# Last rows of wo on half of the partitions, results in two transfers, semaphores cleared, last K in halves

## The chip, the cores and the metric

The kernel runs on one core of a Trainium2 chip. The metric is the device time of one execution, in microseconds (us), lower is better. Before the change three runs took 1300.05, 1300.1 and 1302.17 us; the median is 1300.1 us.

## The reference

One decode step for two tokens (B = 2) of width 512: attention over a cache of 8192 keys in 32 heads of 128, times a gate that comes from a small MLP, plus the input.

```python
def _A_ref(x, k_cache, v_cache, wq, wo):          # x [2,1,512], caches [2,32,8192,128] float32
    q = (x @ wq).reshape(B, Sq, H, Dh).transpose(0, 2, 1, 3)
    scores = jnp.einsum("bhqd,bhkd->bhqk", q, k_cache) * (Dh ** -0.5)
    p = _softmax(scores, axis=-1)
    o = jnp.einsum("bhqk,bhkd->bhqd", p, v_cache)
    return o.transpose(0, 2, 1, 3).reshape(B, Sq, H * Dh) @ wo      # wo [4096, 512]

def _B_ref(x, w1, b1, w2, b2):
    y = _layernorm(x)
    h = _gelu(jnp.einsum("bsd,df->bsf", y, w1) + b1)
    return jnp.einsum("bsf,fd->bsd", h, w2) + b2

xn = _layernorm(x)
return x + _A_ref(xn, k, v, wq, wo) * _silu(_B_ref(xn, w1, b1, w2, b2))
```

All of it is float32. The two caches are 512 MiB together, and each of their values is used once.

## The kernel before

**Blocks.** The 64 pairs of token and head are worked on two at a time: 32 blocks (`N`, index n), each with one K tile and one V tile of 128 partitions x 16384 floats, which is 8 MiB. Half of the partitions belongs to each head of the pair. K tiles alternate between two buffers (`kb[0]`, `kb[1]`); V tiles go to one buffer (`vb`). In the last block V goes to `kb[1]` instead, in two halves (lines 606 to 608), because the wo matrix then needs `vb`.

**One block.** VectorE (DVE) multiplies the K tile with the query, in place and in two halves of 64 keys for each partition (`scores_mul`, L524), and sums each half over the head's 128 values (`scores_sum`, L531). The largest score of each head is found by DVE (L535), turned by TensorE (PE, L538) and reduced again (L541). ScalarE (ACT) takes the exponentials (L552). PE multiplies them with the V tile (`weighted`, L569: 32 matmuls of 512 columns, each of which is two passes in the trace), ACT copies the sums out of PSUM (L574), PE folds them (L576), and DVE spreads them into a matrix `Z` (L582). Blocks are staggered: the V product of block n-1 runs while DVE works on the scores of block n. Blocks 1 to 30 are a hardware loop; the first and the last are written out.

**Transfers.** All large loads are issued by SyncE (SP), in one queue and in the order of the program (`load`, L314). Each waits until its buffer is free: a K load for the scores of the tile before it, a V load for the matmuls of the block before. `load_k` (line 316) takes K tile 0 in two halves, each with a semaphore of its own, so that DVE can start on the first half; all the other K tiles are one transfer. An edit to `load_k` also changes the semaphores' names.

**Order of the work.** `Plan` records every operation with what it reads and writes. It adds the waits that follow from that and writes out each engine's instructions in program order. [...]

**The end (lines 611 to 660).** Once the last V product of `vb` is done, wo is loaded into `vb`: partition p holds rows 32p to 32p+31, 2 KB each. "Column c" below is row 32p+c of every partition, 128 rows and 256 KB in all. The 32 columns come in five transfers, `wo0` to `wo4`, with columns 0-15, 16-25, 26-29, 30 and 31. After the last block, PE and DVE make the normalised attention output `on` (L624 to L629), 128 partitions x 32 columns for each token. The product with wo then has three parts:

- columns 0 to 25 by one matmul of 512 output columns each, summed in four PSUM strips (`wide`, L639), which ACT copies out (L642);
- columns 26 to 29 by four matmuls of 128 output columns each, straight into the final layout (`acc`, L648);
- four matmuls that fold `wide` into `acc` (L653), then columns 30 and 31 as the four before (L648).

DVE multiplies with the gate (L657) and adds x (L658), and SP writes the result with one transfer (L659, 4 x 2 x 128 floats). `emit` ends SP's instructions with a wait for that transfer (L125). Nothing clears the kernel's semaphores.

Of the kernel before, what the change touches and what calls it, by code (L numbers as in the profile page):

```python
# [21 lines left out]
class Plan:  # L22
# [63 lines left out]
    def emit(self, heads):  # L86

        nc = self.nc
# [28 lines left out]
        for e in self.eng:  # L117
            ops = [o for o in self.ops if o.eng == e]
            inside = [j for j, o in enumerate(ops) if o.loop]
            if not inside:  # L120
                for o in ops:
                    put(o, order(o.waits))
                if e == "sp":

                    nc.sync.wait_ge(sems[("dma", "out")], told[("dma", "out")])  # L125
                continue
            for o in ops[:inside[0]]:
                put(o, order(o.waits))
# [32 lines left out]
            for o in ops[inside[-1] + 1:]:  # L161
                put(o, order(o.waits))


def decode_kernel(nc, x, kc, vc, wq, wo, w1, b1, w2, b2, out):
    P = 128
# [17 lines left out]
    RM = RB * (B - 1) + 1  # L184
    PH = P // H
    OC = DH // PH
    UP = U * PH


# [9 lines left out]
    def pe(fn, r=(), w=(), it=None, loop=False):  # L199
        op("pe", fn, r, w, it=it, loop=loop)  # L200

    def dve(fn, r=(), w=(), it=None, loop=False):
        op("dve", fn, r, w, it=it, loop=loop)

    def act(fn, r=(), w=(), it=None, loop=False):
        op("act", fn, r, w, it=it, loop=loop)
# [4 lines left out]
    def sbuf(name, shape):  # L211
        return nc.alloc_sbuf_tensor(name, shape, F32).ap()
# [39 lines left out]
    RS = sbuf("rs", [P, 1])  # L252
    O4 = sbuf("o4", [P, JW * DH])
    q_nat = O4
    rl = sbuf("rl", [P, B])
    on = sbuf("on", [P, RM, OC])

# [45 lines left out]
    def bank():  # L303
        i = turn[0] % 4
        turn[0] += 1
        return scratch[i], f"s{i}"
# [6 lines left out]
    def load(dst, src, sem, w, over=()):  # L313
        op("sp", lambda: nc.sync.dma_start(dst, src), (), w, over=over, dma=sem)  # L314

    def load_k(n):
        i = (n + 1) % 2
        if n == 0:
            for s in range(2):
                load(kbuf[i][:, s * M:(s + 1) * M], kf[n][:, s * M:(s + 1) * M], f"k{s}", [("kb", i, s)])  # L320
            return
        load(kbuf[i], kf[n], f"kb{i}", [("kb", i, s) for s in range(2)])


    WO_PIECES = (0, 16, 26, 30, 31, 32)
    WIDE = WO_PIECES[2]


    load(w1_sb, w1.rearrange("(p c) f -> p c f", p=P), "w1", ["w1"])
# [51 lines left out]
    for j in range(QT):  # L381
# [6 lines left out]
                                        axis=AX.X, op=ALU.add), ["ident"], ["mod"])  # L388
    dve(lambda: nc.vector.tensor_reduce(out=blk, in_=ident.rearrange("p (j r) -> p j r", r=R),
                                        axis=AX.X, op=ALU.add), ["ident"], ["blk"])  # L390
    layernorm(y, xn, "y", "xn", 1)
    transposed(xnT[:, :, (NQ - 1) * B:NQ * B], xn, "xnT", "xn")
    transposed(yT, y, "yT", "y")
# [214 lines left out]
                load(kbuf[1][:, s * M:(s + 1) * M], vf[N - 1][:, s * M:(s + 1) * M], f"v1{s}", [("kb", 1, s)])  # L608


    wo_r = wo.rearrange("(p c) n -> p c n", p=P)
    for i, (a, e) in enumerate(zip(WO_PIECES, WO_PIECES[1:])):
        load(wo_sb[:, a:e], wo_r[:, a:e], f"wo{i}", [("wo", i)], over=["vb"])
# [19 lines left out]
    def piece(c):  # L633
        return ("wo", max(i for i, a in enumerate(WO_PIECES[:-1]) if a <= c))


    for c in range(WIDE):
        j = c % QT
        pe(lambda c=c, j=j: matmul(wide[R * j:R * j + RM, :], on[:, :, c], wo_sb[:, c, :],  # L639
                                   start=(c < QT), stop=(c + QT >= WIDE)), ["on", piece(c)], ["wide"])  # L640
    w4 = O4
    act(lambda: nc.scalar.copy(w4, wide), ["wide"], ["o4"])  # L642

# [1 line left out]
    def rows(lo, hi):  # L645
        for c in range(lo, hi):
            for j in range(QT):
                pe(lambda c=c, j=j: matmul(acc[R * j:R * j + RM, :], on[:, :, c], wo_sb[:, c, j * P:(j + 1) * P],  # L648
                                           start=(c == WIDE), stop=(c == OC - 1)), ["on", piece(c)], ["acc"])

    rows(WIDE, WO_PIECES[3])
    for j in range(QT):
        pe(lambda j=j: matmul(acc[R * j:R * j + RM, :], mod[:, :RM], w4[:, j * P:(j + 1) * P], start=False, stop=False),  # L653
           ["mod", "o4"], ["acc"])
    rows(WO_PIECES[3], OC)

    dve(lambda: nc.vector.tensor_mul(gate, acc, gate), ["acc", "gate"], ["gate"])  # L657
    dve(lambda: nc.vector.tensor_add(gate, gate, x4), ["gate", "x4"], ["gate"])  # L658
    op("sp", lambda: nc.sync.dma_start(out.rearrange("b o (j n) -> j (b o) n", n=P), gate[::RB, :]),  # L659
       ["gate"], dma="out")  # L660

    plan.emit(HEADS)

# [24 lines left out]
```

## Time and profile before

| What | Value |
|---|---|
| Median of three runs | 1300.1 us |
| The profiled execution | 1300.12 us |
| Its span, first to last instruction | 1298.4 us |
| DVE busy | 1134.7 us (87%) |
| PE busy (matmul) | 406.5 us (31%) |
| ACT busy | 77.6 us (6%) |
| Read from HBM | 559.30 MB, 431 GB/s over the span |
| Last instruction of `acc` ends | 1295.92 us |
| SP issues the result | 1296.63 us, takes 0.70 us |
| SP sees it landed | 1298.41 us |

Times in traces count from the first instruction of the profiled execution. The 1.7 us between its span and its time lie ahead of the first and behind the last instruction. PE's matmuls are pipelined: the start of a pass and the distance to the next one say how fast PE goes, while a pass of 512 columns shows 0.59 us of its own. "PEclk" is the share of the full TensorE clock that the chip granted.

The load of a transfer is shared by up to 16 DMA engines. Each reports the end of its share, so the trace has as many completion marks for a transfer as engines took part (one more when fewer than 16 do), and the transfer has landed at the last of them.

| Transfer | Issued at | First mark | Last mark (landed) |
|---|---|---|---|
| K of block 31 | 1194.42 | 1235.03 | 1236.95 |
| V of block 30 | 1227.53 | 1254.38 | 1256.32 |
| V of block 31, first half | 1227.90 | 1264.09 | 1266.02 |
| V of block 31, second half | 1233.10 | 1273.81 | 1275.73 |
| wo0, 16 columns | 1265.66 | 1283.52 | 1285.46 |
| wo1, 10 columns | 1266.03 | 1289.62 | 1291.56 |
| wo2, 4 columns | 1266.50 | 1292.10 | 1294.06 |
| wo3, 1 column | 1266.99 | 1292.79 | 1294.67 |
| wo4, 1 column | 1267.45 | 1293.45 | 1295.30 |

### The profile page before, as it was taken

To read this page: it belongs to the slowest core of one execution; us is meant where nothing else is said; L and a number is where in the kernel's file an instruction comes from. 1 tells how busy PE (TensorE), PEld (TensorE's weight loads), DVE (VectorE), ACT (ScalarE), POOL (GpSimd) and SP (SyncE) were. 2 spreads that over 40 slices of the span, in tenths; PEclk is the share of its full clock that TensorE was granted. 3 is DMA by queue.
4 is the path that set the end of the run, shared out by engine and by line. 5 is a ranking of instruction groups with operands and counts; after the bars stand their busy time and mean duration, and the time that the engine had idled before them with its cause. 6 is when DMAs were issued, how large, how long until landed. Compare 5 with 4: busy or idle time off the path is not lost.

```text
span 1298.4 us, 6747 instructions
## 1 busy us (share of the span) xinstructions
PE 406.5 (31%) x2708; PEld 122.9 (9%) x2708; DVE 1134.7 (87%) x276; ACT 77.6 (6%) x250; POOL 1.4 (0%) x8
## 2 busy tenths in 40 slices
PE   5502333312333311333321333321333321233336
PEld 1100011000101000101100101000101100001102
DVE  3599999888889988889988888988888988888982
ACT  1100000000000000000000000000000000000000
POOL 0000000000000000000000000000000000000000
PEclk9856666556666556666555666655666655666658
DMA  9999999999999999999999999999999999999998
GB/s 404 447 423 444 426 438 432 424 444 428 440 428 432 440 424 444 426 440 430 426 442 428 442 428 434 436 424 444 426 442 428 428 444 424 442 428 436 434 422 358
DMA packets 10682, 559.39 MB, mean 431 GB/s; under 512 B 1192, under 2 KB 1200, under 8 KB 1460
## 3 DMA queue, kind: packets, MB, share of 16 engines
q1 hardware_dynamic: 10668, 559.29, 99.6%
q8 instruction: 4, 0.07, 0.0%
q14 instruction: 2, 0.02, 0.0%
q10 hardware_dynamic: 8, 0.01, 0.0%
HBM read 559.30 MB, written 0.00 MB: 431 GB/s over the span
## 4 chain that ended last, share of the span: by engine, by line
DMA 73%; PE 25%; DVE 1%; issue 0%; ACT 0%; SPq 0%; DVEq 0%
DMA vb<-in_A_v_cache_dram 71%; PE po L569 22%; DMA vb<-in_A_wo_dram 2%; PE s L410 1%; PE po L482 1%; PE s L452 0%; PE wide L639 0%; PE s L412 0%; DVE vb L418 0%; PE acc L648 0%; ACT L431 0%; DVE vb L356 0%; PE s L459 0%; DVE vb L367 0%; DVE vb L444 0%
## 5 line engine op out<-in xcount | busy, mean ns | idle before, releaser
L524 DVE TENSOR_TENSOR kb<-kb,Q 128x8192 f32<-128x8192 f32 x64 | 555.6, 8681 | 109.8 <-DMA kb<-in_A_k_cache_dram 100.5
L531 DVE TENSOR_REDUCE sc<-kb 128x64 f32<-128x8192 f32 x64 | 552.3, 8666 | 0.0
L569 PE MATMUL po<-vb,PZ 128*8 128x512 f32 x1984 | 287.6, 745 | 292.5 <-DMA vb<-in_A_v_cache_dram 292.5
L547 PE MATMUL s<-nm,srow 1*128 1x2 f32 x64 | 18.6, 358 | 368.5 <-DVE nm L541 368.5
L569 PEld LDWEIGHTS po<-vb,PZ 128*8 128x8 f32 x1984 | 57.0, 104 | 497.0 <-issue 494.4
L538 PE MATMUL s<-ident,mx 128*1 128x128 f32 x32 | 11.9, 373 | 186.3 <-DVE mx L535 186.3
L547 PEld LDWEIGHTS s<-nm,srow 1*128 1x128 f32 x64 | 15.9, 307 | 378.0 <-DVE nm L541 378.0
L574 ACT COPY o<-po 128x512 f32<-128x512 f32 x32 | 18.7, 585 | 539.1 <-PE po L569 539.1
L548 ACT COPY bias<-s 128x2 f32<-128x2 f32 x32 | 5.1, 160 | 620.3 <-PE s L547 620.3
L576 PE MATMUL s<-mod,o 128*128 128x2 f32 x256 | 33.7, 254 | 22.8 <-ACT o L574 22.8
L576 PEld LDWEIGHTS s<-mod,o 128*128 128x128 f32 x256 | 31.0, 191 | 52.5 <-ACT o L574 52.5
L552 ACT ACTIVATE PZ<-sc,bias 64x128 f32<-64x128 f32 x64 | 25.5, 399 | 1.8
L538 PEld LDWEIGHTS s<-ident,mx 128*1 128x1 f32 x32 | 2.5, 79 | 189.8 <-DVE mx L535 159.1
L582 DVE TENSOR_TENSOR Z<-blk,s 128x8 f32 (+1 forms) x32 | 5.2, 163 | 12.4 <-PE s L576 12.4
L418 DVE COPY vb<-vb 2x384 f32<-2x384 f32 x4 | 1.8, 502 | 15.1 <-ACT vb L414 15.1
L410 PE MATMUL s<-vb 128*2 128x512 f32 (+1 forms) x24 | 11.7, 638 | 0.3 <-ACT vb L375 0.3
L552 ACT ACTIVATION_READ_ACCUMULATOR PZ<-sc,bias 64x1 f32 x64 | 11.8, 185 | 0.0
L535 DVE TENSOR_REDUCE mx<-sc 128x1 f32<-128x128 f32 x32 | 9.2, 286 | 1.1
L556 ACT ACTIVATE ZR<-half,rs 128x8 f32 (+1 forms) x32 | 9.7, 302 | 4.1
L541 DVE TENSOR_REDUCE nm<-s 1x2 f32<-1x128 f32 x32 | 8.7, 272 | 0.4 <-PE s L538 0.4
L569 PE MATMUL po<-kb,PZ 128*8 128x512 f32 x64 | 8.5, 694 | 1.4 <-ACT PZ L552 1.4
L657 DVE TENSOR_TENSOR gate<-acc,gate 128x128 f32<-128x128 f32 x1 | 0.3, 291 | 9.6 <-PE acc L648 9.6
(86 smaller groups left out, 78.8 us busy)
## 6 DMA issues: line engine op xcount, KB each, us to landing
kb<-in_A_k_cache_dram SPq DMA_DIRECT2D x2, 4096.0 KB, 49.2
kb<-in_A_v_cache_dram SPq DMA_DIRECT2D x2, 4096.0 KB, 40.4
vb<-in_B_w_dram SPq DMA_DIRECT2D x2, 2752.0 KB, 12.7
vb<-in_A_wo_dram SPq DMA_DIRECT2D x1, 4096.0 KB, 19.8
vb<-in_A_wo_dram SPq DMA_DIRECT2D x1, 2560.0 KB, 25.5
vb<-in_A_wo_dram SPq DMA_DIRECT2D x1, 1024.0 KB, 27.6
vb<-in_A_wo_dram SPq DMA_DIRECT2D x2, 256.0 KB, 27.8
kb<-in_A_k_cache_dram SPq DMA_DIRECT2D x31, 42.6
```

The costliest lines, as they stand in the source:

```text
L410: pe(lambda f=f, w=w, ph=ph, c=c: matmul(ph[:B, :w], yT[:, c, :], w1_sb[:, c, f:f + w], start=(c == 0), stop=False), ["yT", "w1"], [k])
L482: pe(lambda i=i, c=c, wv=wv, a=a, j=j, hd=hd: matmul(PO[R * j:R * j + NQ * B, :].rearrange("m (h d) -> m h d", d=DH), xnT[:, c, a:a + NQ * ...
L524: vector(n, n, lambda n: nc.vector.tensor_tensor(out=k, in0=k, in1=cols(Q, n * DH, DH).unsqueeze(1).to_broadcast([P, M, DH]), op=ALU.mult) ...
L531: vector(n, n, lambda n: nc.vector.tensor_reduce(out=SC[:, s * M:(s + 1) * M], in_=k, axis=AX.X, op=ALU.add), [("kb", i, s)], [("sc", s)])
L535: vector(n, n, lambda n: nc.vector.tensor_reduce(out=MX, in_=SC, axis=AX.X, op=ALU.max), [("sc", 0), ("sc", 1)], ["mx"])
L538: pe(lambda i: transpose(PM[:1, :P], MX, ident), ["mx", "ident"], ["s1"], it=n, loop=n > 0)
L547: pe(lambda i: matmul(PN[:, :U], srow, NM, start=True, stop=True), ["srow", "nm"], ["s2"], **one)
L552: act(lambda i, r=r, s=s: nc.scalar.activation(PZ[r, :, s, :], sc[r], AF.Exp, bias=BIAS[r, s:s + 1], scale=SCALE, accum_out=RS[r]), ["bias ...
L556: act(lambda i: nc.scalar.activation(cols(ZR, i * UP - UP, UP), half, AF.Copy, scale=RS), ["half"] + [("rs", s) for s in range(U)], [("ZR" ...
L569: pe(lambda i, t=t, j=j, v=v: matmul(PO[R * j:R * j + U * JW, :], PZ[:, t].rearrange("p s j -> p (s j)"), v[:, t * JW:(t + 1) * JW, :].rea ...
L574: act(lambda i: nc.scalar.copy(O4, PO), ["po"], ["o4"], **one)
L576: pe(lambda i, k=k: matmul(PT[:, :U], O4[:, k * DH:(k + 1) * DH], mod[:, k:U * JW:JW], start=(k == 0), stop=(k == JW - 1)), ["o4", "mod"], ...
```

## The change

- **wo.** Column 31 is no longer the last transfer. It is loaded ahead of the others by two transfers `wx0` and `wx1` (128 KB each) into 64 partitions of the query buffer `Q`, which is free once DVE has multiplied the last K tile. The source is written with a leading dimension of 8. `wo0` to `wo4` now hold columns 0-15, 16-24, 25-28, 29 and 30. As the 64 partitions hold other rows than `on` does, two small matmuls with a selection matrix `pick2` (made once at the start by a DVE copy) bring the matching values into 64 partitions, ACT copies them to `on2`, and two matmuls of 512 columns join the `wide` sum behind columns 0 to 15.
- **Results.** One transfer for each token, one issued by SP and one by ACT, 4 x 128 floats each.
- **Semaphores.** SP waits for both and then clears the kernel's semaphores.
- **Last K.** K tile 31 is loaded in two halves, as K tile 0 is.

```diff
-                if e == "sp":
-                    nc.sync.wait_ge(sems[("dma", "out")], told[("dma", "out")])
...
+        ids = sorted(s.num for s in sems.values())
+        for k in sorted(k for k in sems if k[0] == "dma" and k[1].startswith("out")):
+            nc.sync.wait_ge(sems[k], told[k])
+        nc.sync.sem_clear(range(ids[0], ids[-1] + 1))
...
+    HALF = P // 2
+    EG = 8
...
+    wx = Q[:HALF, :2 * D].rearrange("p (t n) -> p t n", t=2)
+    on2 = sbuf("on2", [HALF, 2, RM])
+    pick2 = sbuf("pick2", [P, 2, HALF])
...
-        if n == 0:
+        if n in (0, N - 1):
             for s in range(2):
-                load(kbuf[i][:, s * M:(s + 1) * M], kf[n][:, s * M:(s + 1) * M], f"k{s}", [("kb", i, s)])
+                load(kbuf[i][:, s * M:(s + 1) * M], kf[n][:, s * M:(s + 1) * M], f"k{i}{s}", [("kb", i, s)])
...
-    WO_PIECES = (0, 16, 26, 30, 31, 32)
+    WO_PIECES = (0, 16, 25, 29, 30, 31)
     WIDE = WO_PIECES[2]
+    LAST = OC - 1
...
+    dve(lambda: nc.vector.tensor_copy(pick2.rearrange("p t (k r) -> p t k r", r=EG),
+                                      ident.rearrange("p (k t r) -> p t k r", t=2, r=EG)), ["ident"], ["pick2"])
...
+    wl = wo.rearrange("(k t r c) n -> t k r c n", t=2, r=EG, c=OC)
+    for t in range(2):
+        load(wx[:, t, :], wl[t, :, :, LAST, :], f"wx{t}", [("wx", t)],
+             over=[("Q", k) for k in range(2 * D // (NB * DH))])
...
-    for c in range(WIDE):
-        j = c % QT
-        pe(lambda c=c, j=j: matmul(wide[R * j:R * j + RM, :], on[:, :, c], wo_sb[:, c, :],
-                                   start=(c < QT), stop=(c + QT >= WIDE)), ["on", piece(c)], ["wide"])
+    p2, k2 = bank()
+    for t in range(2):
+        pe(lambda t=t: matmul(p2[:HALF, t * RM:(t + 1) * RM], pick2[:, t], on[:, :, LAST], start=True, stop=True),
+           ["pick2", "on"], [k2])
+    act(lambda: nc.scalar.copy(on2, p2[:HALF, :2 * RM].rearrange("p (t m) -> p t m", t=2)), [k2], ["on2"])
+    first = [(on[:, :, c], wo_sb[:, c, :], ["on", piece(c)]) for c in range(WIDE)]
+    first[WO_PIECES[1]:WO_PIECES[1]] = [(on2[:, t, :], wx[:, t, :], ["on2", ("wx", t)]) for t in range(2)]
+    for i, (a, b, keys) in enumerate(first):
+        j = i % QT
+        pe(lambda i=i, a=a, b=b, j=j: matmul(wide[R * j:R * j + RM, :], a, b, start=(i < QT),
+                                             stop=(i + QT >= len(first))), keys, ["wide"])
...
-    rows(WO_PIECES[3], OC)
+    rows(WO_PIECES[3], LAST)
...
-    op("sp", lambda: nc.sync.dma_start(out.rearrange("b o (j n) -> j (b o) n", n=P), gate[::RB, :]),
-       ["gate"], dma="out")
+    for b in range(B):
+        eng = "sp" if b % 2 == 0 else "act"
+        op(eng, lambda b=b, eng=eng: plan.eng[eng].dma_start(
+            out[b, 0].rearrange("(j n) -> j n", n=P), gate[RB * b::R, :]), ["gate"], dma=f"out{b}")
```

## The prediction

> **What bounds the kernel now.** I read the page first, for what is busy all the time.
>
> ```profile
> span 1298.4 us, 6747 instructions
> ...
> DMA  9999999999999999999999999999999999999998
> ...
> q1 hardware_dynamic: 10668, 559.29, 99.6%
> ...
> DMA 73%; PE 25%; DVE 1%; issue 0%; ACT 0%; SPq 0%; DVEq 0%
> ```
>
> SP's queue keeps the 16 DMA engines moving for 99.6% of the span. DVE is the busiest compute engine (87%), but it waits 3.5 us for each K tile. The change leaves the bytes as they are, so it can only act on what comes before the first and after the last byte. The end is therefore read next, in the chain of waits from 1227 us on:
>
> ```profile
> 1266.03 25.53 DMA vb<-in_A_wo_dram
> 1291.56 0.04 issue
> 1291.60 2.79 PE wide L639 x19
> 1294.39 0.88 PE acc L648 x32
> 1295.26 0.22 PE acc L653 x7
> 1295.48 0.48 PE acc L648 x16
> ```
>
> From the landing of wo1 at 1291.56 PE goes on until 1295.92. The trace's completion marks show a second chain beside it, hardly shorter: wo4 lands at 1295.30 and PE loads the first weights of column 31 at 1295.41, so the last landing has 0.11 us to spare. The end is set by both.
>
> How unevenly the DMA engines finish is in the windows of the last microseconds (columns: stretch, its length, busy us of PE, PEld, DVE, ACT, POOL, granted clock, DMA share, GB/s):
>
> ```profile
> 1292.00:1293.00 1.00, 1.00 (x16) 0.36 (x10) 0.00 (x0) 0.00 (x0) 0.00 (x0) 1.00 1.05 410
> 1293.00:1294.00 1.00, 1.00 (x12) 0.18 (x4) 0.00 (x0) 0.00 (x0) 0.00 (x0) 1.00 0.48 178
> 1294.00:1295.00 1.00, 1.00 (x34) 0.89 (x32) 0.00 (x0) 0.57 (x1) 0.00 (x0) 1.00 0.13 49
> ```
>
> The share falls from all engines to two. The sixteen marks of wo4 lag behind its first (1293.45) by 0, 0.11, 0.16, 0.26, 0.28, 0.30, 0.38, 0.40, 0.51, 0.60, 0.75, 1.00, 1.03, 1.53, 1.58 and 1.85 us. Five engines are late by 1 us or more. The same lags stand in every V transfer for hundreds of microseconds, so an engine that fell behind stays behind.
>
> **wo over eight engines.** In this trace the number of engines is that of a transfer's leading rows: the result (4 rows) has four completions, x (2 rows) two. So wx, with a leading 8, goes over eight. One column (256 KB) over sixteen engines costs each 0.63 us (wo3 to wo4 lands 0.63 apart); the same bytes over eight cost each of these 1.26. In front of the last landing the eight loaded engines then have 1.26 - 0.63 = 0.63 us more work than before, the other eight 0.63 less. What that gives depends on who is late:
> - latest (1.85) loaded: last landing +0.63;
> - latest not loaded, but 1.53 or 1.58 is: 1293.45 + 1.58 + 0.63 = 1295.66, +0.36;
> - none of these three loaded: 0.63 less for the latest is 1294.67, but a loaded engine with lag 0.75 now ends at 1294.83, -0.47.
>
> The trace names no engine. The packets of x, b1 and b2, on one and two engines, can be followed to the engines with lags 0.60 and 0.75; if the small counts always take the same first engines, these two are loaded. Six more of fourteen are, and were the lags strewn by chance, the three cases had 0.43, 0.42 and 0.15. I take +0.36, from -0.47 to +0.63. If eight engines don't reach their full rate, wx costs up to twice as much (the bound is mine: half rate), +1.26 more.
>
> [...]
>
> **PE behind wo1.** `wide` has one column less to do after wo1: two passes of 0.107 us (at full clock the timeline has four weight loads of L639 every 0.43 us): -0.21 on the first chain. The two wx columns are added ahead of wo1, +0.43, and the selection (4 short passes of 0.03 as in L648, an ACT copy of 0.16 to 0.27 as L548 and L384) ahead of `wide`. PE has idled there for 1.38 us (1290.22 to 1291.56), which covers 0.43; without that cover it would cost in full. The selection is done while PE waits for wo0.
>
> **Last K in halves.** V of block 31 in halves takes 9.70 + 9.71 us between landings, whole tiles 19.35: +0.06 for all engines, on the path. For DVE it takes a wait away:
>
> ```profile
> 1233.10 0.29 DVE L535 TENSOR_REDUCE mx<-sc 128x1 f32<-128x128 f32 x1
> 1233.32 0.16 DVE L582 TENSOR_TENSOR Z<-blk,s 128x8 f32 x1
> 1236.98 8.69 DVE L524 TENSOR_TENSOR kb<-kb,Q 128x8192 f32<-128x8192 f32 x1 [3.50 <-DMA kb<-in_A_k_cache_dram]
> ...
> 1271.68 0.29 DVE L535 TENSOR_REDUCE mx<-sc 128x1 f32<-128x128 f32 x1
> ```
>
> The first half lands near 1227.3, so L524 starts at 1233.5, 3.45 us earlier; the second half is there at 1237, before DVE needs it at 1242.2. Everything to `on` follows: 1271.68 becomes 1268.2, L569 starts at 1271.3, its second half needs V landed at 1275.8 and PE is there at 1276.3, `on` is ready at 1283.0 instead of 1286.42. There the gain stops: wo0 lands at 1285.5 or later. It isn't on the path (0), and it has an effect of its own: PE stands still from 1282.5 until wo0.
>
> **PE's clock.** What such a rest does is in the windows of the clock's own 3.41 us steps:
>
> ```profile
> 1226.58:1229.99 3.41, 1.93 (x20) 0.97 (x8) 3.41 (x1) 0.58 (x1) 0.00 (x0) 1.00 1.02 442
> 1229.99:1233.41 3.42, 0.00 (x0) 0.00 (x0) 3.39 (x3) 0.00 (x0) 0.00 (x0) 0.50 1.06 460
> ...
> 1274.37:1277.78 3.41, 3.05 (x16) 0.64 (x20) 0.00 (x0) 0.52 (x3) 0.00 (x0) 0.50 1.05 452
> 1277.78:1281.19 3.41, 3.41 (x36) 0.83 (x32) 0.00 (x0) 0.00 (x0) 0.00 (x0) 1.00 1.02 437
> ...
> 1288.02:1291.43 3.41, 2.20 (x23) 0.54 (x14) 0.00 (x0) 0.00 (x0) 0.00 (x0) 1.00 0.92 388
> ```
>
> A step with PE busy for 1.93 us is followed by half clock, one with 2.20 is not; a step of 3.05 us at half clock brings full clock back. PE's rest of 3 to 4 us always leaves one step under 1.9. So `wide` starts at half clock, 0.213 us a pass (four of L569 every 0.85 us), and gets it back after 3.4 us (6 chances in 10 by where the steps lie) or 5.2 to 6.5: 1.7 us lost, or 2.6 to 3.2. With a late engine loaded (lag 1.66 at wo0), wo0 lands at 1283.52 + 1.66 + 1.26 + 0.06 = 1286.50. Then 36 passes are through at 1286.57 + 3.85 + 1.7 = 1292.1, wo1 is there (1291.95), 18 passes more take 1.93: the last starts at 1294.1 instead of 1293.80. First chain: +0.3, or up to +1.5 with the longer half clock. The last landing gives +0.36 + 0.06 - 0.11 = +0.3 too. I take +0.3.
>
> **Two results.** The issue of 4 x 2 x 128 took 703 ns; transfers with one dimension less took 433 (wo2) on SP and 541 (x) on ACT. Both run side by side, the later decides: 0.541 - 0.703 = -0.16, I take -0.15; bounds -0.37 (328, the shortest) to +0.3 (four engines serve two queues; the marks of the one before lie 0.61 to 0.68 behind the first).
>
> **Semaphores.** Nothing hides this; it is SP's last instruction. SP's shortest there is 17 ns (L125), its longest without a wait 703: 0.02 to 0.70, I take 0.05, by the row that also only touches semaphores.
>
> [...]
>
> **Others, at nothing.** `pick2` is one DVE copy of 128 x 128 (0.37 as L387 at most), ahead of a DVE idle of 8.24 us and of K tile 0, behind which SP's queue is full until 56 us. SP's wx issues (2 x 0.43) stand before wo0's and wait for DVE's last L524, which ends near 1251; wo0 waits until 1265.66 anyway. Is wx late, wo0 to wo4 are late behind it; it isn't, by 14 us.
>
> **Sum.** +0.3 - 0.15 + 0.05 = +0.2. The sum is made against the profiled execution, 1300.12 with a span of 1298.4, which is 0.02 from the median: 1300.3 us.
>
> **Rivals.**
> 1. Eight engines at half rate and `wide` at half clock (slower). If the latest is loaded, wo0 lands at 1285.46 + 2.52 + 0.06 = 1288.0, PE starts cold there, and 32 + 4 + 18 passes with 3.4 to 6.8 us of half clock start the last one at 1295.5 to 1297.2, +1.7 to +3.4. With the other terms 1301.7 to 1303.4; it counts as slower from the long half clock on. For it: the clock rows, nothing else in the change is as large. Against: the 2 KB packets of wo3 and wo4 take 84 to 93 ns each in the trace, with other engines idle or not. 1302.7, chance 0.12.
> 2. The late engines are all among those relieved, and `wide` isn't last (faster, a little): -0.47 + 0.06 - 0.11 = -0.5, with -0.1 for the rest 1299.5. Chance 0.2. Against: chance alone gives 0.15. For: five lags over 1 us, none of them on the two engines that I could follow.
> 3. wx goes over all sixteen after all: columns only change places, +0.06 - 0.1, 1300.1. Against: the result's four completions. Chance 0.06.
>
> The forecast, 1299.9 to 1301.6, has the remaining 0.62.
>
> **How the numbers follow.** A measurement of this kernel can tell 0.2% from no change, 2.6 us. All terms at their best give -0.5 - 0.37 + 0.02: 1299.3. At their worst, without rival 1's half rate, +1.65 (latest loaded, long half clock) + 0.3 + 0.7: 1302.8. That is the range, 1299.2 to 1302.8. Faster by 2.6 us is more than the whole of the lags (1.85) could give: 0.04, for what I don't see. Slower by 2.6: most of rival 1, and SP's clear at its bound on top of the longer half clock, 0.11. Same: 0.85.
>
> **What would show it.** Steps right: completions of wx eight (nine marks); its issue near 1251; first L524 of block 31 at 1233.5; `on` 3.4 us earlier; half clock at the start of `wide`; wo4's landing within 0.7 of 1295.3; two issues at the end under 0.6 us each; one more instruction behind SP's last wait. The prediction is wrong if the landing of wo4 moves by over 1 us, if SP's clear takes over 0.7, or if the time outside the span changes.

## The result, and the profile after

| | Before | After |
|---|---|---|
| Median (lowest to highest, 22 runs each) | 1301.16 us (1299.89 to 1303.10) | 1303.24 us (1302.47 to 1304.37) |
| Ratio, after to before | | 1.0016, 95% interval 1.0010 to 1.0022 |
| The profiled execution | 1300.12 us | 1303.06 us |
| Its span | 1298.4 us | 1301.7 us |
| Time outside the span | 1.7 us | 1.3 us |
| wo4 landed | 1295.30 us | 1296.99 us |
| Last instruction of `acc` ends | 1295.92 us | 1298.84 us |

The kernel is slower by 2.1 us of 1301, or 0.16%. That is less than the 0.2% that the prediction took as the least that a measurement can tell, but the interval lies wholly above 1. The predicted 1300.3 us and its range, up to 1302.8, are both missed. The two profiled executions lie 2.94 us apart, more than the medians, because the profiled one of the kernel before is among its fastest. What follows explains the 2.94 us.

First the page of after, its span and its share of DMA (40 slices), then the chain of waits (start us, us, what):

```profile
span 1301.7 us, 6766 instructions
...
DMA  9999999999999999999999999999999999999997
```

```profile
1266.16 21.59 DMA vb<-in_A_wo_dram
1287.76 0.04 issue
1287.80 8.77 PE wide L666 x52
1296.57 0.35 PE acc L675 x8
1296.92 0.40 PE wide L666
1297.31 0.88 PE acc L675 x22
1298.19 0.22 PE acc L680 x8
1298.40 0.48 PE acc L675 x15
```

The chain has changed its shape. Before, it ran from the landing of wo1 and PE had idled ahead of that. Now it leaves the transfers at the landing of wo0 (1287.76, 1285.46 before), and PE then works without a break to 1298.84. It works slowly: 8.77 us for 52 passes, which at the 0.107 us of full clock are 5.6. The end is 2.92 us later, the landing of wo4 only 1.69. So two things have to be explained: transfers that land late, and a slow PE behind them.

**The transfers.** Windows of the kernel after around wx (stretch, length, busy us of PE, PEld, DVE, ACT, POOL, granted clock, DMA share, GB/s):

```profile
1273.00:1274.00 1.00, 1.00 (x12) 0.31 (x8) 0.00 (x0) 0.00 (x0) 0.00 (x0) 0.50 1.03 360
1274.00:1275.00 1.00, 1.00 (x12) 0.18 (x7) 0.00 (x0) 0.00 (x0) 0.00 (x0) 0.50 0.73 193
1275.00:1276.00 1.00, 1.00 (x12) 0.21 (x8) 0.00 (x0) 0.00 (x0) 0.00 (x0) 0.89 1.49 434
1276.00:1277.00 1.00, 1.00 (x14) 0.12 (x8) 0.00 (x0) 0.00 (x0) 0.00 (x0) 1.00 0.77 258
1277.00:1278.00 1.00, 1.00 (x12) 0.22 (x8) 0.00 (x0) 0.00 (x0) 0.00 (x0) 1.00 0.93 393
```

The last two columns are read together: the engines are busy (share 0.73 to 1.49, about 1 on average), but the bytes fall from 430 to 193 and 258 GB/s. The engines are at work and move little, so something holds them up. The records of single packets say the same. Those of wx, 2 KB each, take 84 to 271 ns; the 2 KB packets of wo3 and wo4 take 84 to 96. And the 32 KB packets that start from 1274 to 1277 take 1302 to 1869 ns, where 1213 to 1222 stood before. These packets belong to V and wo0, not to wx: the slow transfer slows the others beside it (with column 31 loaded as a plain column they take 1213 to 1247, a_plain below). The second half of V lands at 1276.69 (1275.73 before), and wo0 to wo4 1.7 to 2.3 us later than before.

**PE.** The same view of the kernel after, cut at the clock's own steps:

```profile
1282.05:1285.46 3.41, 1.39 (x13) 1.18 (x12) 0.56 (x3) 0.18 (x1) 0.00 (x0) 1.00 0.96 415
1285.46:1288.87 3.41, 1.07 (x8) 0.37 (x12) 0.00 (x0) 0.00 (x0) 0.00 (x0) 0.50 0.95 404
1288.87:1292.28 3.41, 3.41 (x21) 0.73 (x16) 0.00 (x0) 0.00 (x0) 0.00 (x0) 0.50 0.94 399
1292.28:1295.69 3.41, 3.41 (x29) 0.72 (x24) 0.00 (x0) 0.00 (x0) 0.00 (x0) 1.00 0.73 291
```

PE rests from 1283.96 to 1287.80. The step in which the rest begins has 1.39 us of work and is followed by half clock; the next has 1.07 and is followed by half clock again; the one after is full and brings the clock back at 1292.28. `wide` falls into these two steps, as the timeline of PE shows (start us, us, operation, and in brackets the wait ahead):

```profile
1287.80 5.84 PE L666 MATMUL wide<-vb,on 128*17 128x512 f32 x32 [3.84 <-DMA vb<-in_A_wo_dram]
1293.57 1.04 PE L666 MATMUL wide<-Q,on 64*17 64x512 f32 x4
1294.54 2.35 PE L666 MATMUL wide<-vb,on 128*17 128x512 f32 x17
```

The first 32 passes take 5.84 us. Before, at full clock, they took 3.65:

```profile
1286.57 3.65 PE L639 MATMUL wide<-vb,on 128*17 128x512 f32 x32 [0.61 <-DVE on L629]
```

And the four passes of wx, with the clock back, take 0.97 us from their start to the next (1293.57 to 1294.54), where four passes of 128 rows start every 0.43 us.

**What went as foreseen.** DVE takes the last K tile when its first half is there, and everything up to `on` moves forward (start us, us, engine, line, operation):

```profile
1233.59 8.69 DVE L538 TENSOR_TENSOR kb<-kb,Q 128x8192 f32<-128x8192 f32 x1
...
1283.27 0.22 DVE L647 TENSOR_TENSOR on<-OA,rl 128x64 f32<-128x64 f32 x1
```

The multiplication starts 3.39 us earlier, and `on` is there at 1283.49 (1286.42 before). And the end of the kernel after has its two transfers of results: SP issues one at 1299.55 in 0.59 us, and ACT the other at nearly the same time in 0.61 us. SP's has landed at 1301.20, ACT's at 1301.57, and the clear ends at 1301.73.

### The profile page after: what moved, and what is told of

Same layout as the page of the kernel before. It is cut to its first block, busy times and chain, and to the rows that moved or that the text cites. A ratio compares the mean times of both kernels' runs of the same rounds, so it can differ in the third digit from the quotient of the medians.

```text
span 1301.7 us, 6766 instructions
## 1 busy us (share of the span) xinstructions
PE 406.1 (31%) x2714; PEld 122.9 (9%) x2714; DVE 1134.7 (87%) x277; ACT 77.9 (6%) x251; POOL 1.4 (0%) x8
## 4 chain that ended last, share of the span: by engine, by line
DMA 73%; PE 25%; DVE 1%; issue 0%; ACT 0%; SPq 0%; DVEq 0%
DMA vb<-in_A_v_cache_dram 72%; PE po L583 22%; DMA vb<-in_A_wo_dram 2%; PE s L424 1%; PE wide L666 1%; PE po L496 1%; PE s L466 0%; PE s L426 0%; DVE vb L432 0%; PE acc L675 0%; ACT L445 0%; DVE vb L368 0%; PE s L473 0%; DVE vb L379 0%; DVE vb L458 0%
## 5 line engine op out<-in xcount | busy, mean ns | idle before, releaser
L583 PE MATMUL po<-vb,PZ 128*8 128x512 f32 x1984 | 282.7, 734 | 294.9 <-DMA vb<-in_A_v_cache_dram 294.9
L549 DVE TENSOR_REDUCE mx<-sc 128x1 f32<-128x128 f32 x32 | 9.2, 287 | 1.1
L666 PE MATMUL wide<-vb,on 128*17 128x512 f32 x50 | 8.6, 790 | 3.8 <-DMA vb<-in_A_wo_dram 3.8
```

The costliest lines, as they stand in the source:

```text
L583: pe(lambda i, t=t, j=j, v=v: matmul(PO[R * j:R * j + U * JW, :], PZ[:, t].rearrange("p s j -> p (s j)"), v[:, t * JW:(t + 1) * JW, :].rea ...
L666: pe(lambda i=i, a=a, b=b, j=j: matmul(wide[R * j:R * j + RM, :], a, b, start=(i < QT), stop=(i + QT >= len(first))), keys, ["wide"])
```

## The experiments

All runs below are timed against the kernel before on the same chip, 11 runs of the kernel (4 in one case) against 21 to 33. "Median span" is the middle one of the spans of a kernel's runs; it was 1301.8 us for the kernel after and 1298.5 to 1299.1 for the kernel before.

### Which part of the change costs

**a_kwhole: the kernel after, K tile 31 whole again.**

```diff
-        if n in (0, N - 1):
+        if n == 0:
```

> The changed kernel with K tile 31 in one transfer again. Clock theory (the rest of PE that the earlier scores leave before wo0 costs full clock): on is ready near 1286.5, PE rests about 1 us before wo0, wide starts at full clock (36 passes in 3.9 us instead of 6.8), the last instruction of acc ends 1.0 to 1.4 us earlier, near 1297.5, and the span falls from 1301.7 to 1300.3 to 1300.7. Rival (only the late landing of wo4, 1296.99, sets the end): on later, wide at whatever clock, span within 0.3 of 1301.7.

1303.57 us, ratio 1.0016 (1.0007 to 1.0025), as slow as the kernel after; the median span is 1302.2. `on` is late again (1286.77). `wide` now starts at full clock, at 1287.72, but loses it at 1288.86 for one step of 3.41 us, so that its first 32 passes still take 5.36 us (columns as above):

```profile
1288.00:1290.00 2.00, 2.00 (x16) 0.52 (x12) 0.00 (x0) 0.00 (x0) 0.00 (x0) 0.71 0.99 420
```

In the step before that PE is busy for 2.39 us: with the small matmuls of the last fold and the selection, and with only the first passes of `wide`, as wo0 lands at 1287.67. With K whole and wo0 on time `wide` keeps the full clock (its first 32 passes take 3.65 us in the kernel before and 3.66 in b_out below). So the halves of K are not needed for the half clock: a late wo0 brings it too.

**b_khalf: the kernel before with K tile 31 in halves.** The same two lines, put into the kernel before.

> The kernel before with K tile 31 in two halves and nothing else. Clock theory: on near 1283, wo0 lands at 1285.5, PE rests 2.6 us, wide starts at half clock; as wo1 lands only at 1291.6, at most 0.5 us of the loss reaches the end: span 1298.4 to 1299.1. Landings later by 0.05 to 0.15. Rival (the halves are worth something by themselves): span 0.3 or more below 1298.4.

1300.56 us, ratio 0.9998 (0.9989 to 1.0007). Here is PE in it (start us, us, operation, and in brackets the wait ahead):

```profile
1285.73 5.50 PE L639 MATMUL wide<-vb,on 128*17 128x512 f32 x32 [2.01 <-DMA vb<-in_A_wo_dram]
1291.84 2.78 PE L639 MATMUL wide<-vb,on 128*17 128x512 f32 x20 [0.61 <-DMA vb<-in_A_wo_dram]
```

The rest is there and so is the half clock (5.50 us), but PE is through before wo1 lands and waits 0.61 us for it. (`on` is there at 1284.19 and wo4 lands 0.21 later than before, both later than expected.) So the halves do make a rest and a half clock, as the prediction had it. The half clock alone costs nothing as long as wo0 is on time.

**a_plain: the kernel after with column 31 loaded first as an ordinary column** (128 partitions, sixteen engines), without the selection. Halves of K, results and clear stay.

```diff
-    wx = Q[:HALF, :2 * D].rearrange("p (t n) -> p t n", t=2)
+    wx = Q[:, :D]
...
-    for t in range(2):
-        load(wx[:, t, :], wl[t, :, :, LAST, :], f"wx{t}", [("wx", t)],
+    load(wx, wo.rearrange("(p c) n -> p c n", p=P)[:, LAST, :], "wx", ["wx"], over=[("Q", 0)])
```

> The changed kernel with column 31 still loaded first, but as an ordinary column: 128 partitions, sixteen engines, one matmul in wide, no selection. Theory (eight engines into 64 partitions hold up everybody): the 2 KB packets take 84 ns again and the 32 KB packets beside them 1213 instead of 1430 to 1870, the lags of wo0 are those of V again (no second group 1.4 us behind), wo4 lands 0.9 to 1.5 us earlier than the 1296.99 of the changed kernel. PE still starts wide at half clock, so the span falls by less, to 1300.2 to 1301.2. Rival (only the clock sets the end): span within 0.3 of 1301.7.

1300.26 us, ratio 0.9994 (0.9985 to 1.0003). Packets of 2 KB are at 84 to 92 ns, those of 32 KB at 1213 to 1247, wo4 lands at 1295.39. The whole loss is gone with this one edit, more than was expected: the median span is 1298.9, where 1300.2 was the least that the expectation allowed. The edit also takes the passes of 64 rows out of `wide`, which the last part of this section prices.

**b_wx: the kernel before with the new wx and its selection alone.**

> The kernel before with the new wx and its selection alone: last K whole, one transfer of the results, no clear. If wx alone carries the loss (theory A with D): wo4 at 1296.8 to 1297.1, wide's first 32 passes 5 us or more, the span 2.3 to 2.9 us longer than the 1298.4 of before, time 1302.6 to 1303.6. If the two results or the clear carry a part of it that matters: 1301.5 to 1302.3.

1303.62 us, ratio 1.0014 (1.0005 to 1.0023); wo4 at 1297.14, the first 32 passes in 5.99 us, span 1301.6. With +3.2 the profiled span is a little over the expected 2.9. `on` is late as well in this kernel (1287.35), but `wide` starts at 1287.95, right behind the landing of wo0 (1287.90). The clock is at half for the 4.78 us behind that. wx alone makes the loss, and it makes the half clock with it, as K is whole here.

**b_out: the kernel before with two transfers of the results and the clear alone.**

> The kernel before with the two transfers of the results and the clear alone. By the kernel after, where 2.18 us lie between the issue and the end instead of 1.80 and 1.33 us outside the span instead of 1.69: span 0.3 to 0.45 us longer; time 0.0 to 0.1 us longer if the time outside the span shrinks with it (theory F: the clear inside the span takes over work that was done behind it), 0.3 to 0.45 us longer if it does not (theory G: the 1.33 us of the kernel after came from its code being fetched earlier).

1301.18 us, ratio 0.9999 (0.9990 to 1.0008). In the profile SP sees both landed 1.96 us behind its issue (1.78 before), and the clear ends 0.15 us after that, of which the instruction itself takes 0.076. So from the issue to the end it is 2.11 us instead of 1.80, +0.3 in the span. The time outside the span is not shorter (median 1.88 us, 1.75 for the kernel before beside it): theory F fell.

**a_act: the kernel after with the copy to `on2` on DVE and both results issued by SP**, so that ACT has the instructions of before.

```diff
-    act(lambda: nc.scalar.copy(on2, p2[:HALF, :2 * RM]...
+    dve(lambda: nc.vector.tensor_copy(on2, p2[:HALF, :2 * RM]...
...
-        eng = "sp" if b % 2 == 0 else "act"
+        eng = "sp"
```

> The changed kernel with ACT's instructions as before: DVE copies on2, both results are issued by SP. Theory (ACT's three added instructions push its code over a block, and the 8 KB fetch at 1272.3 takes 0.67 us from the latest DMA engine): no instruction fetch between 100 and 1280 us, the second half of V lands 0.6 earlier (1276.0), the time outside the span is 1.7 again instead of 1.3; the second result lands 0.3 to 0.6 later, as its issue waits for the first. Span 1301.0 to 1301.8. Rival (another engine's code): the fetch stays near 1272.

1303.22 us, ratio 1.0015 (1.0006 to 1.0024). ACT has no part in it. An 8 KB packet of instructions that comes at 1272.3 in the kernel after is still there at 1272.4. It isn't needed for the loss: a_kwhole and b_wx are as slow, and theirs comes at 1300.9 and 1301.6.

### Why wx is slow

By then wx was known to be the cause. Theory A puts it where the engines write, B where they read, C down to the small number of engines.

**a_ports: wx in four transfers of 32 partitions.** With the rows dealt out in equal shares over eight engines, which the trace does not name, engine i writes the partitions 4i to 4i+3 and, in the next transfer, those 32 further on.

```diff
-    EG = 8
+    EG = 4
...
-    for t in range(2):
-        load(wx[:, t, :], wl[t, :, :, LAST, :], ...
+    for t in range(2):
+        for hf in range(2):
+            load(wx[hf * R:(hf + 1) * R, t, :], wl[t, hf, :, :, LAST, :], ...
```

> The kernel after with wx in four transfers of 32 partitions instead of two of 64: each engine then writes four partitions in a row instead of eight, and no two of the eight engines write within the same group of partitions p and p + 32 in one transfer. Bytes per engine, selection and results stay. Theory A (the eight engines of the kernel after get in each other's way at the writing end, as their packets' 112 to 271 ns instead of 84 and the other engines' 1430 to 1869 ns instead of 1213 suggest): the 2 KB packets are back at 84 to 95 ns, the second half of V 31 lands by 1276.0 (1276.69), wo4 at 1295.9 to 1296.3 (1296.99), and the time is 1301.7 to 1302.5. Theory B (it is the reading end: rows a megabyte apart per engine) and theory C (it is that few engines carry it, however they are placed): packets as slow as in the kernel after, wo4 at 1296.8 to 1297.2, time 1303.0 to 1303.5.

1301.37 us, ratio 1.0005 (0.9996 to 1.0014), a little faster than theory A expected. 2 KB packets at 84 to 94 ns, V landed at 1275.68, wo4 at 1295.99. The packets decide for theory A. The rows read and the eight engines are those of the kernel after, so B and C have fallen as causes of what a_ports takes away.

**a_contig: wx from rows that lie one behind the other.** It reads the first 128 rows of wo in place of column 31.

```diff
-wl[t, :, :, LAST, :]
+wo[t * HALF:(t + 1) * HALF, :].rearrange("(k r) n -> k r n", r=EG)
```

> The kernel after with wx read from the first 128 rows of wo, which lie one behind the other in memory, in place of every 32nd row; which engines carry it and where it lands are unchanged. Its sum over wo thus takes other rows for column 31. Theory B (the reading end): 2 KB packets at 84 to 95 ns, wo4 at 1295.9 to 1296.3, time 1301.7 to 1302.5. Theories A (the writing end) and C (few engines): nothing changes, wo4 at 1296.8 to 1297.2, time 1303.0 to 1303.5.

1303.54 us, ratio 1.0020 (1.0011 to 1.0029). One assumption of the expectation was wrong: two dimensions that lie one behind the other are merged into one of 64 rows when the program is built, and the transfer went over sixteen engines (sixteen marks). It is slow all the same (packets up to 244 and 2356 ns), so reading in order doesn't help.

**a_sixteen: groups of four rows, sixteen engines, 64 partitions.**

```diff
-    EG = 8
+    EG = 4
```

> The kernel after with groups of four rows instead of eight: wx still lands on 64 partitions in two transfers, but over sixteen engines, four partitions each, so that engines i and i + 8 write partitions 32 apart. Seventeen marks where there were nine. Theory C (few engines, and their lead and lag over the others): free of it, wo0 in one group of lags, wo4 at 1295.3 to 1295.7 as with the plain column (1295.39), time 1300.1 to 1300.9. Theory A in its form of shared partitions p and p + 32: all sixteen engines meet in pairs, their packets stay at 150 ns or more, wo4 at 1295.9 to 1296.5, time 1301.0 to 1302.0. Theory B: the rows lie as far apart as before, packets slow on all sixteen, the same 1301.0 to 1302.0.

1302.91 us, ratio 1.0012 (1.0003 to 1.0021), wo4 at 1296.51. Sixteen marks, and still slow, by more than the 1302.0 us at most that was expected: 2 KB packets at up to 181 ns, those of 32 KB at 1573 to 1816. Theory C fell, theory A in the form with p and p + 32 stands.

**a_rows8: the plain column, its source grouped in 16 times 8 rows.**

```diff
-wo.rearrange("(p c) n -> p c n", p=P)[:, LAST, :]
+wo.rearrange("(k r c) n -> k r c n", r=EG, c=OC)[:, :, LAST, :]
```

> The run with the plain column (column 31 on 128 partitions over sixteen engines, 1300.26 us), with one thing changed: the source is grouped in 16 times 8 rows, so that each engine takes eight partitions in a row. Bytes, engines, packets for each engine, rows read and place in SBUF are the same; only which engine writes which partition changes. Theory A (engines meet where they write, since each has partitions of its own in an ordinary transfer and loses them when eight in a row are dealt out): packets of 2 KB at 100 to 270 ns instead of 84, packets of 32 KB next to them at 1400 us-thousandths (ns) or more instead of 1213, wo4 at 1296.0 to 1297.1 instead of 1295.39, time 1301.0 to 1303.0. Theory C (too few engines or half of the partitions) and theory B (the reading end): as the plain column, wo4 at 1295.3 to 1295.6, time 1300.0 to 1300.7.

1300.73 us, ratio 0.9992 (0.9983 to 1.0001), packets as in a_plain. This says nothing against A: the two dimensions have been merged again, and the built instruction is the plain column's, 128 rows of 512. It is a second measurement of that kernel.

**a_off0 and a_off: the four transfers of a_ports, and the same four partitions further on.** The selection is widened to 128 partitions in both; they differ in one number.

```diff
-    OFF = 0
+    OFF = 4
```

> The kernel after with wx in four transfers of 32 partitions, as in the run that took them to partitions 0 to 63 (1301.37 us), with the selection widened to 128 partitions (rows 64 to 127 of it are zero), so that it can be compared with its twin four partitions further on. As that run: packets of 2 KB at 84 to 95 ns, packets of 32 KB at 1213 to 1250, wo4 at 1295.9 to 1296.3, time 1300.9 to 1301.9.

> The same with all of wx four partitions further on (4 to 67 instead of 0 to 63): same engines, packets, rows read, groups of four partitions for each engine. Theory A (in the ordinary transfers each engine writes partitions that no other engine writes to at that place, four in a row and the four that lie 32 behind; wx is slow when an engine's partitions are another engine's): now each engine writes where its neighbour's packets go, so packets of 2 KB at 100 ns or more, packets of 32 KB at 1400 ns or more beside them, wo4 at 1296.5 to 1297.2, time 1302.0 to 1303.6. Theory H (eight partitions in a row for one engine are slow by themselves, four in a row are not, wherever they lie): as its twin, 1300.9 to 1301.9.

a_off0 1300.66 us, ratio 1.0000 (0.9991 to 1.0009); a_off 1302.28 us, ratio 1.0013 (1.0004 to 1.0022). On the same chip the slowest run of a_off0 (1301.46) is faster than the fastest of a_off (1301.75). The windows of a_off0, then those of a_off:

```profile
1273.00:1275.00 2.00, 2.00 (x16) 0.37 (x12) 0.00 (x0) 0.00 (x0) 0.00 (x0) 0.50 0.94 390
1275.00:1277.00 2.00, 2.00 (x21) 0.42 (x17) 0.00 (x0) 0.00 (x0) 0.00 (x0) 0.97 0.98 413
1277.00:1279.00 2.00, 2.00 (x24) 0.52 (x20) 0.00 (x0) 0.00 (x0) 0.00 (x0) 1.00 1.18 508
```

```profile
1273.00:1275.00 2.00, 2.00 (x16) 0.37 (x12) 0.00 (x0) 0.00 (x0) 0.00 (x0) 0.69 0.89 266
1275.00:1277.00 2.00, 1.47 (x16) 0.22 (x12) 0.00 (x0) 0.00 (x0) 0.00 (x0) 1.00 1.10 281
1277.00:1279.00 2.00, 2.00 (x24) 0.56 (x20) 0.00 (x0) 0.00 (x0) 0.00 (x0) 1.00 0.87 305
```

The share of busy DMA is much the same, the bytes differ by a third (last column), and wo4 lands at 1296.07 and at 1297.67 (more than the 1297.2 expected at most). Four partitions in a row are no help by themselves: theory H fell. What counts is where the groups lie: four partitions further on, the packets of wx take 133 ns in the median instead of 84, and those of 32 KB 1968 instead of 1221. In a_off no two engines of one wx transfer write 32 partitions apart, so meeting each other in pairs isn't needed: by theory A they meet the packets of V and wo0. That a start at partition 4 costs by itself was not tried; the kernel after and a_sixteen start at 0 and are slow too.

Kernels side by side, from the packet records (2 KB: the packets of wx; 32 KB: those that start from 1274 to 1277 us; ns, median and longest):

| Kernel | Engine i writes | 2 KB | 32 KB | wo4 landed |
|---|---|---|---|---|
| before | no wx | | 1213, 1222 | 1295.30 |
| a_plain | as in the other transfers | 84, 92 | 1221, 1247 | 1295.39 |
| a_ports | 4i to 4i+3, then + 32 | 84, 94 | 1221, 1248 | 1295.99 |
| a_off0 | the same | 84, 93 | 1221, 1248 | 1296.07 |
| a_off | the same, + 4 | 133, 185 | 1968, 2198 | 1297.67 |
| a_sixteen | 4i to 4i+3, i up to 15 | 102, 181 | 1682, 1816 | 1296.51 |
| a_contig | the same | 138.5, 244 | 2008, 2356 | 1297.07 |
| after | 8i to 8i+7 | 121, 271 | 1713, 1869 | 1296.99 |

Which engine takes which partitions isn't in the trace; the second column is inferred from the order of the rows in the instruction, dealt out in equal shares. By it a_contig and a_sixteen differ only in the rows that they read, and the one that reads in order is the slower; whether the reading end adds to the cost stays open. What the table shows is the place: the four transfers of a_ports and a_off0 run like a plain column (2 KB packets at 84 ns in the median), and the same groups + 4, or 64 partitions in a row over eight or sixteen engines, do not (102 to 138.5). Theory A is the author's explanation and agrees with every row; that engines meet where they write is not seen in a trace.

### What the clock adds

**a_warm: sixteen matmuls that nobody reads, ahead of `wide`.**

```diff
+    for i in range(16):
+        pe(lambda: matmul(p3[:RM, :], on[:, :, LAST], kb[0][:, :D], start=True, stop=True), ...
```

> The kernel after with 16 matmuls of 512 columns whose result nobody reads, ahead of the first pass of wide, behind the selection, so that PE does not rest between 1284 and 1288. Theory D (PE's rest halves its clock for the first passes of wide, and that costs what the landing of wo4 alone does not explain, about 1.3 us): the first 32 passes take 3.6 to 4.0 us instead of 5.84, the last matmul of acc ends 2.1 to 2.4 us behind the landing of wo3 and wo4 allows, at 1297.3 to 1297.7 instead of 1298.84, time 1301.7 to 1302.2. Theory E (the end is set by the landings alone): time as the kernel after, 1303.0 to 1303.5.

1314.48 us (4 runs), ratio 1.0103. The price was wrong by four: the passes of `wide` go to four strips and run four at a time, four every 0.43 us at full clock; these all went to one, at 0.43 to 0.85 us each, and took 15.19 us. It tests nothing, but it gave the size for the next.

**a_warm2: three of them.**

```diff
+    for w in (512, 512, 256):
+        pe(lambda w=w: matmul(p3[:RM, :w], on[:, :, LAST], kb[0][:, :w], start=True, stop=True), ...
```

> The kernel after with three matmuls whose result nobody reads (512, 512 and 256 columns, six instructions one behind the other, at 0.43 us or, at half clock, 0.85 us each by the run with sixteen of them) between the selection and wide: they end near 1287.4, before wo0 lands, and fill the step of the clock from 1284.7 to 1288.1. Theory D (PE's rest from 1284 to 1287.8 halves its clock for the first passes, and this costs what the landings alone do not explain): the first 32 passes of wide take 3.6 to 4.2 us instead of 5.84, the last matmul of acc ends 0.6 to 0.8 us behind the landing of wo4 (1.85 in the kernel after), at about 1297.6 instead of 1298.84, and the time is 1301.7 to 1302.3. Theory E (the landings alone set the end): 1303.0 to 1303.5.

1302.11 us, ratio 1.0006 (0.9997 to 1.0015), median span 1300.8 against 1301.8 of the kernel after, while wo4 lands as late (1297.13). That speaks for D and against E, though the intervals of the two ratios (1.0010 to 1.0022 for the kernel after) still overlap. But the added matmuls did not do what was expected of them: the first 32 passes still needed 5.1 us, and `acc` ends 1.12 us behind wo4, not 0.6 to 0.8. The clock's steps in a_warm2:

```profile
1279.92:1283.33 3.41, 2.70 (x24) 1.85 (x16) 0.16 (x1) 0.58 (x1) 0.00 (x0) 1.00 0.99 418
1283.33:1286.75 3.42, 2.90 (x9) 0.94 (x9) 0.40 (x2) 0.18 (x1) 0.00 (x0) 0.50 0.95 407
1286.75:1290.16 3.41, 3.41 (x15) 0.81 (x17) 0.00 (x0) 0.00 (x0) 0.00 (x0) 0.51 0.98 418
1290.16:1293.57 3.41, 3.41 (x29) 0.77 (x21) 0.00 (x0) 0.00 (x0) 0.00 (x0) 1.00 0.95 395
```

Here the clock's steps lie otherwise than in the profile of the kernel after. The clock goes down at 1283.33 instead of 1285.46, before the added matmuls begin, and comes back two steps on, at 1290.2 instead of 1292.3. So the run has 2 us more of full clock in `wide`, and a median span 1.0 us shorter; that the added matmuls brought it about isn't shown, as the place of the steps alone can shift it.

**What sets the end, from the traces of the other runs.** Take the seven kernels with wx passes of 64 rows and no added matmuls (after, a_kwhole, b_wx, a_act, a_ports, a_contig, a_sixteen). In each, `acc` ends 8.80 to 8.85 us behind the first pass of `wide`, plus half of the time that the clock is at half behind that pass (4.49 us of it in the kernel after, 3.47 in a_act, 2.80 in a_ports). So PE sets their end, 1.00 to 2.00 us behind the landing of wo4, and theory E falls. (A pass at half clock takes twice as long, 0.213 us in place of 0.107.) In a_off0, where the wx passes have 128 rows, the same sum has 7.71 us in place of 8.80.

For the kernel after this gives estimates. By the landings alone it would have ended at 1296.99 + 0.62 = 1297.61 (0.62 us lie between wo4 and the end before, 0.63 in a_off); PE adds 1.23 us. At full clock PE would have been through at 1296.60, and with passes of 128 rows at 1297.75. Each of the two alone would have been hidden behind the late wo4, or nearly so. Together they cost the 1.23 us.

## Why the prediction was wrong

**wo over eight engines: the step that failed.** It took eight engines to run at their full rate, made the last landing later by +0.36 (from -0.47 to +0.63), and kept the half rate for rival 1 and out of the range. Measured: +1.69. Of this, a_ports shows the part that the step had priced: with packets at full rate wo4 lands 0.69 later, the case "latest loaded" (+0.63 and the 0.06 of the halves). The other 1.00 comes with the slow packets. The step argued against it with "the 2 KB packets of wo3 and wo4 take 84 to 93 ns each in the trace, with other engines idle or not". That row was true but for its end (84 to 95 by the records) and did not bear on the case: those are columns over 128 partitions and sixteen engines (sixteen marks each), and no transfer of the trace before has the form of wx. The half rate was the author's own bound. No run shows it: where wx is slow its packets take 102 to 138.5 ns in the median, and half rate would be twice 84. And it was thought of as a price for wx alone; that the 32 KB packets of V and wo0 would take 1302 to 1869 ns was not foreseen at all. The lower bound had a slip too: -0.47 leaves out the engines with lags 1.00 and 1.03, of which a loaded one would end at 1295.11, -0.19.

**Rival 1 came out in its numbers, and in part by luck.** It put wo0 at 1288.0 (measured 1287.76), the start of the last pass at 1295.5 to 1297.2 (1296.72) and the time at 1302.7 (1303.24 median, 1303.06 profiled). The half clock and the slow eight engines were there. But the packets of wx took 125 ns in the mean, not twice 84, which makes 0.65 us for each of its engines where the rival had 1.26. The rest came from the slow packets of V and wo0, which the rival did not have.

**PE's clock: right mechanism, too small in the sum.** `wide` started at half clock. The forecast let it last 3.4 us behind the start of `wide` and the landing of wo1 hide most of it; it lasted 4.5 us (1287.80 to 1292.28), and nothing hid it. The first chain was to end 0.3 us later and ended 2.92 later, 1.23 of it more than the landing of wo4 explains. In a_ports PE sets the end as well, at 1296.99: `wide` starts 1.01 us earlier there, and 2.80 instead of 4.49 us of half clock behind its start make the other 0.84. How much of this 0.84 comes with the late wo0, and how much from where the clock's steps happen to lie, isn't shown.

**PE behind wo1 (-0.21) and the wx passes (+0.43, hidden).** The cover was the idle 1.38 us ahead of wo1. In the kernel after there is none: PE never waits for wo1 (landed 1293.26, used at 1294.54), so the wx passes are paid in full. They are also dearer than priced. Call four passes that start together a slot. The slot before them starts at 1293.03 and the one behind them at 1294.54, which is 1.08 us more than the 0.43 between two slots. With 64 rows they went two at a time (1293.57 and 1294.01) and not beside passes of 128 rows; in a_off0, with 128 rows, wx passes start together with those of wo1, four every 0.43 us. The selection was hidden, as foreseen (1283.55 to 1284.2, wo0 lands at 1287.76).

**Last K in halves.** As predicted: the first multiplication at 1233.59 (1233.5), the maximum of the scores (L549, L535 before) at 1268.29 (1268.2). `on` is 0.5 us later than the 1283.0; the late V does not explain that, as a_ports and a_plain have V by 1275.71 and `on` only at 1283.9. Alone it costs nothing (b_khalf). It does make PE's rest and a half clock, as the forecast said (b_khalf), but it isn't the only thing that does: with K whole the late wo0 brings the half clock too (a_kwhole, b_wx).

**Two results: mis-sized.** The issues are shorter, 0.59 and 0.61 us instead of 0.70, but that the lost dimension does it isn't shown: in b_wx the one transfer of before was issued in 0.62 us. And the taken -0.15 is +0.25 in the kernel after (SP sees the landing 2.03 us behind the issue, 1.78 before) and +0.18 in b_out. The bound of +0.3, "four engines serve two queues", held.

**Semaphores.** The clear takes 0.078 us (0.05 taken), and 0.05 us lie between it and the wait ahead.

**Outside the span.** Taken as unchanged, and named as a sign of error: it went from 1.7 to 1.3 us, a gain of 0.4 that hides a part of the loss. It is 1.32 to 1.40 in the median of all kernels with column 31 loaded first, b_wx among them, and 1.73 to 1.88 in before, b_khalf and b_out. In the first group the last 8 KB packet of instructions starts no later than 0.02 us behind the span's end, in the second 1.0 to 1.15 us behind it. That this fetch is the difference is argued from that, not tested.

**Sum.** 2.92 at the end of `acc` (1.69 by the landing of wo4, 1.23 by PE), 0.37 for results and clear, -0.36 outside: 2.93, with 2.94 between the two profiled executions.

## What to carry to other kernels

A transfer into some of the partitions must not be priced by the rate of transfers into all of them (2 KB packets at 121 ns in the median here, 84 in a plain column). Groups of four rows on the partitions 4i to 4i+3, then on those 32 further on, ran at full rate (a_off0), and a shift by four partitions cost 1.6 us (a_off). A price measured on one shape says nothing on another whose condition it lacks, and when the old trace has no transfer of the new shape, that is no reason to give the slow case a small chance. Terms that use the same cover are to be costed together: the half clock alone was hidden in b_khalf, but with a late wo0 and dearer wx passes it was not, and PE added 1.23 us to the 1.69 us of the late landing.

No version beat the kernel before by more than a measurement can tell; the nearest are a_plain (0.9994, 0.9985 to 1.0003) and a_rows8, the same program in its transfers (0.9992, 0.9983 to 1.0001).

## What the runs showed of the hardware that was not expected

- The slow transfers slow engines that carry none of them: in the kernel after all twenty recorded 32 KB packets that start from 1274 to 1277 us are slow (1302 ns or more), though eight of the sixteen engines had no part in wx (wx0 and wx1 have nine marks each). Theory A alone doesn't explain that; it stays open.
- The clock does not go by the busy time of the page alone. In a_warm2 a step with PE busy for 2.70 us, most of it matmuls of 1 to 32 columns, was followed by half clock, and one with 2.90 us at half clock did not bring it back. In a_kwhole a step with 2.39 us at full clock was followed by half clock. The prediction's reading (1.93 is followed by half clock, 2.20 is not, 3.05 brings it back) was too simple.
- Two transfers issued at the same time from SP and from ACT did not land together: their last marks are 0.37 us apart in the kernel after and 0.28 in b_out, and 0.18 to 0.39 us in the other kernels that issue from both.
- Matmuls over 64 rows did not run beside matmuls over 128 in the kernel after: four passes took two slots, and the slot behind them starts 1.51 us after the one before them, where two slots of 128 rows start 0.43 apart.
- Row dimensions of a source that lie one behind the other are merged when the program is built, so a leading dimension that is written down does not always decide how many engines carry a transfer (sixteen marks in a_contig, where eight engines were expected; the plain column's 128 rows in a_rows8).
